# Three instructions reordered in the first dense block, six background VectorE jobs moved later

## The chip, the cores and the metric

The kernel runs on one core of one Trainium2 chip, as one program. Times are device microseconds (us) from the first to the last instruction of the run. The engines are TensorE (PE, with its weight loads as PEld), VectorE (DVE), ScalarE (ACT), GpSimd (POOL) and SyncE (SP, which only issues transfers here).

## The reference, cut to what matters

Three layers follow each other: an attention with two kinds of masks, a gated dense layer, and a layer that sends each token to one of eight experts.

```
scores = scale * np.matmul(q, k.transpose(0, 1, 3, 2))        # q, k, v: 4 x 8 x 576 x 64
scores = np.where(masks[None, :, :, :], scores, -1000000000.0)
attn = np.exp(scores - np.max(scores, axis=-1, keepdims=True))
attn = attn / (np.sum(attn, axis=-1, keepdims=True) + 1e-09)
x = np.matmul(attn, v)            # then laid out as 2304 tokens x 512
...
gate = 1.0 / (1.0 + np.exp(-(x @ w_gate)))                    # w_gate, w_val: 512 x 1536
val = x @ w_val
x = gate * val @ w_out                                        # w_out: 1536 x 512
...
h = np.maximum(xc[mask] @ w1[e], 0.0)                         # per expert e, tokens whose best gate is e
y[mask] = gate_w[mask, None] * (h @ w2[e])
out[do_compute] = xc + y
```

## The kernel before, in words

**Attention.** The work is cut into 32 parts (`NS` = 32, numbered t here): a pair of heads of one batch and half of its rows. A step t of the loop works on four parts at once. TensorE makes the scores of part t (`scores`) and turns the exponentials of part t-2 round (`flip`, L319), and applies v to part t-3 (`apply_v`, L335). VectorE takes the row maxima of part t (L291), adds up and inverts the row sums of part t-1 (L303, L304), copies one of the two turned tiles of part t-2 (`pT`, L321) and the result of part t-3 (L341 or L347). ScalarE makes the exponentials of part t-1 (L297) and copies the other turned tile (L323). GpSimd multiplies both tiles of part t-1 with the inverted sums (`norm`, L310, two instructions that follow each other), and then does one subtraction of two tiles of x (L413). In every second step one more pair of q and k is turned (`turn`, `turn_rest`).

The order in which a step issues its pieces is a string of letters, which is also the order on each engine. It is `eSfEmIFnaNDTMRpDAaL` for t < 32: e and E are the exponentials, S the scores, f and F the two flips with their copies, m and M the two maxima, I the sums and their inverse, n and N the two GpSimd multiplications, T and R the turns, A the application of v, L the loads. The letters D, a and p each take one job from the front of a background queue of VectorE, ScalarE and GpSimd. When the front job's inputs are not there yet, or the queue is empty, nothing is issued.

**Background jobs.** The dense layer multiplies float32 numbers as a high and a low part of each operand. `operand` queues, for each half of a tile of x, a ScalarE job (high part, L425) and a VectorE job that needs it (low part, `xl` = x - `xh`, L429, 128x384, both inputs in SBUF). In the last steps of the attention VectorE's queue holds only such low parts, for the first and second pair of token groups (p = 0 and 1).

**First dense block.** The dense layer runs over 12 blocks of columns (f) and 3 pairs of token groups (p). A block (`Block`) gathers seven products in four PSUM banks A, B, C and D, and each product (`mm`) is six matmuls (L558 to L560). `onto("C", "B")` copies bank B to bank C on ScalarE (L597), where the next product goes on adding; a fresh bank is written once by TensorE first (L564). `keep` copies B to SBUF (L590), `gate_of` takes a sigmoid (L601), `add_d` adds bank D (VectorE, L604). The first block (f = 0, p = 0, `first_period`) is spread over the last steps: each letter G issues one of its pieces. Those steps have strings of their own, for t = 32, 33 and 34 (`NS`, `NS + 1`, `NS + 2`). The rest follows as `period`, block by block, with no attention beside it.

Of the kernel before, what the change touches and what calls it, by code (L numbers as in the profile page):

```python
# [23 lines left out]
def kernel(  # L24
# [626 lines left out]
    def first_period(k):  # L651
        k.mm("A", "A11", "B11", True)
        yield
        k.onto("B", "A")
        k.mm("D", "S3", "T3", True)
        yield
        k.mm("B", "S2", "T2", False)
        k.keep("u2")
        yield
        k.mm("A", "A12", "B21", False)  # L660
        yield
        k.mm("B", "S1", "T1", False)
        k.gate_of("sA", "A")
        k.onto("C", "B")
        k.keep("u4")
        yield
        k.mm("C", "S4", "B22", False)
        k.add_d("u4")
        yield
        k.mm("D", "A22", "T4", False)  # L670
        k.gate_of("sC", "C")
        yield
        k.add_d("u2")
# [8 lines left out]
    NS = len(subs)  # L682
# [68 lines left out]
    def step_fill(t):  # L751
        if not first_block:
            blk0.append(Block(0, 0, lambda _: "X"))
            first_block.append(first_period(blk0[0]))
        next(first_block[0], 0)
# [53 lines left out]
        "D": lambda t: pop("D"), "a": lambda t: pop("A"), "p": lambda t: pop("P"),  # L809
    }  # L810
    ps_of = {}
    ORDERS = {NS: "LeAGEInNDfFapGDa", NS + 1: "LAGGfFGapDDaD", NS + 2: "LGAGGapDDa"}
    for t in range(NS + 3):
        for c in ORDERS.get(t, "eSfEmIFnaNDTMRpDAaL"):
            steps_of[c](t)
# [79 lines left out]
    for f, p in BL:  # L895
# [17 lines left out]
        k = Block(f, p)  # L913
# [22 lines left out]
    def slab(shape, dt, name):  # L936
        return late.tile(shape, dt, tag="slab", bufs=NSLAB, name=name)
# [273 lines left out]
    for i in range(8):  # L1211
        k = (NU - 3) * NC + 6 + 3 * i
# [199 lines left out]
    with tc.For_i(SLOTS, top, 128):  # L1412
# [32 lines left out]
        for e in range(NE):  # L1445
# [21 lines left out]
            for kk in range(KD):  # L1467
                t = slab([128, F], F32, f"ow1{e}{kk}")
# [3 lines left out]
            for i in range(NF // 2):  # L1472
                t = slab([128, 2, DM], F32, f"ow2{e}{i}")
# [47 lines left out]
```

## Time and profile before

| what | value |
|---|---|
| median of 3 runs | 765.17 us (763.15 to 766.51) |
| the profiled execution | 766.11 us, its span 763.9 us |
| TensorE busy | 735.4 us, 96% of the span |
| VectorE, ScalarE, GpSimd busy | 500.7, 417.9, 211.1 us |
| mean granted TensorE clock | 0.992 |

A span counts from the first to the last instruction of the profiled execution; some 2 us lie around it. The attention reaches to about 120 us, the first dense block from there to 134 us, the rest of the dense layer to about 398 us.

### The profile page before, as it was taken

Reading aid. Unit: us, or ns where it says so; the run is one execution under the profiler, and the core shown is the slowest. Engines: PE = TensorE matmul, PEld = TensorE weight load, DVE = VectorE, ACT = ScalarE, POOL = GpSimd, SP = SyncE. Lnnn points to the kernel's source line nnn. Section 1 sums busy time; section 2 is a strip of 40 time slices with the busy share of each in tenths; the row PEclk is TensorE's granted clock in tenths of the full one; section 3 lists DMA queues with packets and bytes.
Section 4 is the critical chain, followed back from the end, with each engine's and each line's share of the span. In section 5 each row is a group of like instructions: output and inputs, shape, how many; then the busy total and the mean of one; then the engine's idle time right before and its main releaser. Section 6 shows DMA issues by size and latency. Waiting matters only on the chain. (4 is left out here: it accounts for less than half of the span.)

```text
span 763.9 us, 13894 instructions
## 1 busy us (share of the span) xinstructions
PE 735.4 (96%) x4773; PEld 670.9 (88%) x4773; DVE 500.7 (66%) x1139; ACT 417.9 (55%) x1153; POOL 211.1 (28%) x233
## 2 busy tenths in 40 slices
PE   8999998999999999999999999999999899999993
PEld 5766666999999999999989999999988788888882
DVE  3799997978877777778656244345555766666540
ACT  5788886755555555555455233344445665566630
POOL 6677976000000000000010020210222755556510
PEclk9999999999999999999999999999999999999997
DMA  9999611243344443443456934626633667777600
GB/s 207 223 210 212 143 32 29 96 146 128 128 149 149 135 144 122 155 139 121 156 182 208 301 122 130 204 94 218 234 124 120 225 244 249 242 227 226 208 16 13
DMA packets 115795, 122.47 MB, mean 160 GB/s; under 512 B 58167, under 2 KB 90679, under 8 KB 115720
## 3 DMA queue, kind: packets, MB, share of 16 engines
q1 hardware_dynamic: 108952, 109.62, 47.2%
q0 software_dynamic: 4000, 8.51, 3.2%
q10 hardware_dynamic: 2768, 3.41, 1.3%
q8 instruction: 39, 0.64, 0.3%
q14 instruction: 36, 0.29, 0.1%
HBM read 90.78 MB, written 36.59 MB: 167 GB/s over the span
## 5 line engine op out<-in xcount | busy, mean ns | idle before, releaser
L558 PE MATMUL psX<-gt,wo 128*128 128x384 f32 x288 | 98.5, 342 | 1.2 <-DVE sl L1144 1.2
L559 PE MATMUL psX<-gt,wo 128*128 128x384 f32 x288 | 96.8, 336 | 0.3
L560 PE MATMUL psX<-gt,wo 128*128 128x384 f32 x288 | 96.4, 335 | 0.0
L609 POOL DMA_DIRECT2D gt<-sC x3 | 1.7, 568 | 256.4 <-DVE sC L607 256.4
L297 ACT ACTIVATE sm<-psX,mx 96x128 f32<-96x128 f32 (+2 forms) x176 | 61.8, 375 | 10.3 <-DVE mx L291 8.0
L310 POOL TENSOR_TENSOR sm<-sm,rs 96x384 f32<-96x384 f32 (+2 forms) x64 | 55.5, 887 | 32.3 <-DVE rs L304 20.3
L604 DVE TENSOR_TENSOR u<-psD,u 128x384 f32<-128x384 f32 x70 | 38.7, 553 | 36.1 <-PE psD L560 34.9
L558 PEld LDWEIGHTS psX<-gt,wo 128*128 128x128 f32 x288 | 54.2, 188 | 1.7 <-DVE sl L1144 1.5
L559 PEld LDWEIGHTS psX<-gt,wo 128*128 128x128 f32 x288 | 54.2, 188 | 1.2 <-DVE gt L874 1.2
L560 PEld LDWEIGHTS psX<-gt,wo 128*128 128x128 f32 x288 | 54.1, 188 | 0.0
L560 PE MATMUL psA<-xhB,wl 128*128 128x384 f32 x140 | 47.0, 336 | 0.7 <-DVE wl L531 0.7
L560 PE MATMUL psD<-xhT,wl 128*128 128x384 f32 x140 | 47.0, 336 | 0.2 <-DVE wl L531 0.2
L990 ACT COPY row<-psY 128x256 f32<-128x256 f32 x36 | 13.4, 373 | 61.5 <-PE psY L988 50.8
L558 PE MATMUL psD<-xhT,wh 128*128 128x384 f32 x140 | 46.9, 335 | 0.0
L559 PE MATMUL psA<-xlB,wh 128*128 128x384 f32 x140 | 46.8, 334 | 0.0
L559 PE MATMUL psD<-xlT,wh 128*128 128x384 f32 x140 | 46.8, 334 | 0.0
L558 PE MATMUL psA<-xhB,wh 128*128 128x384 f32 x140 | 46.8, 334 | 0.0
L560 PE MATMUL psB<-xhT,wl 128*128 128x384 f32 x140 | 46.8, 334 | 0.0
L558 PE MATMUL psB<-xhT,wh 128*128 128x384 f32 x140 | 46.8, 334 | 0.0
L559 PE MATMUL psB<-xlT,wh 128*128 128x384 f32 x140 | 46.8, 334 | 0.0
L991 DVE TENSOR_REDUCE lp<-psY 128x10 f32<-128x40 f32 x36 | 7.2, 199 | 56.4 <-ACT row L990 56.4
L871 ACT CAST gt<-gt 128x384 fp32r<-128x384 f32 x72 | 35.5, 514 | 12.3 <-DMA gt<-gt 10.0
(770 smaller groups left out, 2245.5 us busy)
## 6 DMA issues: line engine op xcount, KB each, us to landing
w1r<-in_moe_w_dram SPq DMA_DIRECT2D x32, 512.0 KB, 5.1
w2r<-in_moe_w_dram SPq DMA_DIRECT2D x32, 512.0 KB, 3.7
gt<-gt SPq DMA_DIRECT2D x72, 192.0 KB, 4.1
gt<-sC SPq DMA_DIRECT2D x33, 192.0 KB, 2.4
gt<-sA SPq DMA_DIRECT2D x33, 192.0 KB, 1.9
wg<-in_moe_w_gate_dram SPq DMA_DIRECT2D x12, 512.0 KB, 4.0
wv<-in_moe_w_val_dram SPq DMA_DIRECT2D x12, 512.0 KB, 3.6
wo<-in_moe_w_out_dram SPq DMA_DIRECT2D x12, 512.0 KB, 3.9
```

The source lines that it names most:

```text
L297: nc.scalar.activation(sm[:n, w, 0:c], src[:, w, :], AF.Exp, bias=mx[:n, w:w + 1], accum_out=sums[:n, h, w:w + 1])
L310: nc.gpsimd.tensor_tensor(x, x, rs[:n, h, 0:m].rearrange("p (w o) -> p w o", o=1).to_broadcast([n, m, c]), op=ALU.mult)
L558: nc.tensor.matmul(ps, lhsT=whi, rhs=xhi, start=start, stop=False, skip_group_check=skip)
L559: nc.tensor.matmul(ps, lhsT=whi, rhs=xlo, start=False, stop=False, skip_group_check=skip)
L560: nc.tensor.matmul(ps, lhsT=wlo, rhs=xhi, start=False, stop=stop, skip_group_check=skip)
L604: nc.vector.tensor_tensor(self.tm[nm], self.ps["D"], self.tm[nm], op=ALU.add)
L609: eng.dma_start(gts[self.f][2 * self.p + i], self.tm[nm])
L871: nc.scalar.copy(t[:, 0, :].bitcast(F32R), t[:, 1, :])
L990: nc.scalar.copy(row[m][:, 256 * a:256 * a + 256].rearrange("p (c n) -> p c n", c=2), pr[:, :, 0:128])
L991: nc.vector.tensor_reduce(lp[:, m, a, :], pr[:, :, 128:NR].rearrange("p c (t n) -> p n c t", t=2), axis=AX.XY, op=ALU.add)
```

## The change

In the first dense block the sigmoid of bank A is issued behind the copy from B to C and behind the copy of B to SBUF. In the steps t = 26 to 31 the letter D between N and T is left out, so that each takes one VectorE job instead of two. The three last strings have four letters D more: t = 32 two, t = 33 and t = 34 one each.

```diff
@@ first_period
         k.mm("B", "S1", "T1", False)
-        k.gate_of("sA", "A")
         k.onto("C", "B")
         k.keep("u4")
+        k.gate_of("sA", "A")
         yield
         k.mm("C", "S4", "B22", False)
         k.add_d("u4")
@@
-    ORDERS = {NS: "LeAGEInNDfFapGDa", NS + 1: "LAGGfFGapDDaD", NS + 2: "LGAGGapDDa"}
+    LATE = "eSfEmIFnaNTMRpDAaL"
+    ORDERS = {t: LATE for t in range(26, NS)}
+    ORDERS.update({NS: "LeAGEInNDDfFapGDDa", NS + 1: "LAGGfFGapDDDaD", NS + 2: "LGAGGapDDDa"})
     for t in range(NS + 3):
         for c in ORDERS.get(t, "eSfEmIFnaNDTMRpDAaL"):
             steps_of[c](t)
```

On ScalarE, at the end of the fifth piece of the first block (psX are its banks A, B and C; u_00 is `u4`, sA and sC are the two sigmoids), the rows with - are before and those with + are after:

```order
 L323 COPY pT<-psY 108x324
+L597 COPY psX<-psX 128x384
+L590 COPY u_00_2378<-psX 128x384
 L601 ACT_TABLE_LOAD
-L601 ACTIVATE sA_2379<-psX 128x384
-L597 COPY psX<-psX 128x384
-L590 COPY u_00_2384<-psX 128x384
-L601 ACTIVATE sC_2411<-psX 128x384
+L601 ACTIVATE sA_2380<-psX 128x384
+L601 ACTIVATE sC_2410<-psX 128x384
 L425 CAST xhT_2440<-xT_1915 128x768
```

The table load of the sigmoid moves with it: both stand behind the two copies now.

On VectorE, the step t = 27 before, from the sums to the copy of part 26's turned tile in the next step (xl are the low parts):

```order
L303 TENSOR_SCALAR sums<-sums 96x6
L304 RECIPROCAL rs<-sums 96x6
L429 TENSOR_TENSOR xlT_1627<-xT_1505,xhT_1626 128x384
L291 TENSOR_REDUCE mx<-psX 96x3
L429 TENSOR_TENSOR xlT_1758<-xT_1646,xhT_1757 128x384
L341 COPY x_1510<-psY 128x192
L341 COPY x_2049<-psY 128x96
L321 COPY pT<-psY 128x288
```

The same place after the change:

```order
L303 TENSOR_SCALAR sums<-sums 96x6
L304 RECIPROCAL rs<-sums 96x6
L291 TENSOR_REDUCE mx<-psX 96x3
L429 TENSOR_TENSOR xlT_1627<-xT_1505,xhT_1626 128x384
L341 COPY x_1510<-psY 128x192
L341 COPY x_2047<-psY 128x96
L321 COPY pT<-psY 128x288
```

The low part between the inverse and the maximum is gone, the one behind the maximum stays, and the jobs come one place later in each of the six steps.

On VectorE, the steps t = 32 and 33 before, from the inverse of the last part to the first addition of the first block:

```order
L304 RECIPROCAL rs<-sums 108x6
L429 TENSOR_TENSOR xlT_2157<-xT_2046,xhT_2156 128x384
L321 COPY pT<-psY 126x252
L429 TENSOR_TENSOR xlT_2271<-xT_2176,xhT_2270 128x384
L347 COPY x_1511<-psY 128x14x6
L347 COPY x_2050<-psY 128x14x12
L321 COPY pT<-psY 108x324
L429 TENSOR_TENSOR xlT_2271<-xT_2176,xhT_2270 128x384
L604 TENSOR_TENSOR u_00_2384<-psX,u_00_2384 128x384
```

The same place after the change:

```order
L304 RECIPROCAL rs<-sums 108x6
L429 TENSOR_TENSOR xlT_1896<-xT_1777,xhT_1895 128x384
L429 TENSOR_TENSOR xlB_1963<-x_969,xhB_1962 128x384
L321 COPY pT<-psY 126x252
L429 TENSOR_TENSOR xlB_1963<-x_969,xhB_1962 128x384
L429 TENSOR_TENSOR xlB_2026<-x_970,xhB_2025 128x384
L347 COPY x_1511<-psY 128x14x6
L347 COPY x_2048<-psY 128x14x12
L321 COPY pT<-psY 108x324
L429 TENSOR_TENSOR xlB_2026<-x_970,xhB_2025 128x384
L429 TENSOR_TENSOR xlT_2154<-xT_2044,xhT_2153 128x384 x2
L429 TENSOR_TENSOR xlT_2266<-xT_2172,xhT_2265 128x384
```

Three low parts have become eight in this place, before the row L604 (the last of nine stands behind the second addition). One of the added ones stands ahead of the copy pT of 126x252, which part 30 needs before v can be applied to it. TensorE's and GpSimd's instructions and all transfers keep their order.

## Rows read from the trace of the kernel before

**Rows 1.** Busy time by stretch: length, PE, PEld, DVE, ACT, POOL, clock, DMA share, GB/s

```profile
97.00:121.00 24.00, 21.75 (x229) 15.48 (x229) 23.01 (x60) 20.48 (x96) 18.16 (x20) 1.00 0.09 26
134.00:398.00 264.00, 262.22 (x1504) 259.97 (x1503) 200.74 (x355) 142.74 (x278) 4.20 (x11) 1.00 0.41 136
```

**Rows 2.** TensorE's waits, 97 to 142 us: waiting row, releaser: total, times, longest

```profile
PE psY L319 <- POOL sm L310: 2.2, 8, 0.3
PE psX L558 <- ACT psX L597: 1.5, 1, 1.5
PE psY L335 <- DVE pT L321: 0.4, 1, 0.4
```

**Rows 3.** ScalarE in order of time: start, duration, instruction, [idle time before, releaser]

```profile
127.60 0.43 ACT L323 COPY pT<-psY 108x324 f32<-108x324 f32 x1 [1.18 <-PE psY L319]
128.05 1.28 ACT L601 ACT_TABLE_LOAD   x1
129.34 0.49 ACT L601 ACTIVATE sA<-psX 128x384 f32<-128x384 f32 x1
129.73 0.49 ACT L597 COPY psX<-psX 128x384 f32<-128x384 f32 x1
130.13 0.48 ACT L590 COPY u<-psX 128x384 f32<-128x384 f32 x1
```

**Rows 4.** TensorE in order of time at the same place

```profile
128.41 0.34 PE L564 MATMUL psX<-xhB,wh 128*128 128x384 f32 x1
130.27 0.44 PE L558 MATMUL psX<-xhB,wh 128*128 128x384 f32 x1 [1.52 <-ACT psX L597]
```

**Rows 5.** VectorE in order of time, step t = 27

```profile
105.50 0.19 DVE L304 RECIPROCAL rs<-sums 96x6 f32<-96x6 f32 x1
105.61 0.51 DVE L429 TENSOR_TENSOR xlT<-xT,xhT 128x384 fp32r<-128x384 f32 x1
106.04 0.55 DVE L291 TENSOR_REDUCE mx<-psX 96x3 f32<-96x384 f32 x1
106.51 1.50 DVE L429 TENSOR_TENSOR xlT<-xT,xhT 128x384 fp32r<-128x384 f32 x1
107.93 0.51 DVE L341 COPY x<-psY 128x192 f32<-128x192 f32 x2
```

**Rows 6.** GpSimd in order of time, step t = 27

```profile
105.86 0.95 POOL L310 TENSOR_TENSOR sm<-sm,rs 96x384 f32<-96x384 f32 x1 [1.08 <-ACT kq L254]
106.77 0.82 POOL L310 TENSOR_TENSOR sm<-sm,rs 96x384 f32<-96x384 f32 x1
107.56 1.31 POOL L413 TENSOR_TENSOR xT<-x,x 128x384 f32<-128x384 f32 x1
```

**Rows 7.** VectorE and GpSimd in order of time, step t = 29

```profile
114.08 0.56 DVE L429 TENSOR_TENSOR xlB<-x,xhB 128x384 fp32r<-128x384 f32 x1
114.19 0.92 POOL L310 TENSOR_TENSOR sm<-sm,rs 126x252 f32<-126x252 f32 x1
114.56 0.51 DVE L341 COPY x<-psY 128x192 f32<-128x192 f32 x2
```

**Rows 8.** VectorE in order of time, the sums of step t = 30

```profile
115.99 0.17 DVE L303 TENSOR_SCALAR sums<-sums 108x6 f32<-108x6 f32 x1 [0.27 <-ACT sm L297]
```

**Rows 9.** VectorE in order of time, steps t = 32 to 34

```profile
122.36 0.54 DVE L303 TENSOR_SCALAR sums<-sums 108x6 f32<-108x6 f32 x1
123.01 0.19 DVE L304 RECIPROCAL rs<-sums 108x6 f32<-108x6 f32 x1
123.11 0.52 DVE L429 TENSOR_TENSOR xlT<-xT,xhT 128x384 fp32r<-128x384 f32 x1
123.55 0.41 DVE L321 COPY pT<-psY 126x252 f32<-126x252 f32 x1
123.88 1.44 DVE L429 TENSOR_TENSOR xlT<-xT,xhT 128x384 fp32r<-128x384 f32 x1
...
130.65 0.56 DVE L604 TENSOR_TENSOR u<-psX,u 128x384 f32<-128x384 f32 x1 [1.99 <-ACT u L590]
```

**Rows 10.** GpSimd in order of time, step t = 32

```profile
124.18 0.72 POOL L310 TENSOR_TENSOR sm<-sm,rs 108x324 f32<-108x324 f32 x1
124.87 1.32 POOL L413 TENSOR_TENSOR xT<-x,xT 128x384 f32<-128x384 f32 x1
```

**Rows 11.** TensorE in order of time, v applied to part 30

```profile
124.02 0.65 PE L335 MATMUL psY<-pT,v 126*64 126x126 f32 x8 [0.40 <-DVE pT L321]
```

## The prediction

> **What bounds the kernel now.** I looked first at the busy times by stretch. From 134 us on TensorE is busy 262.22 of 264 us in the dense layer [rows 1], and its order there is not touched. So the change is worth what it moves the start of that stretch, and no more. Ahead of it, in the last attention steps (97 to 121 us), VectorE is busy 23.01 of 24 us and TensorE 21.75 [rows 1]: VectorE, or what VectorE waits for, sets the pace. Then TensorE's own waits: between 97 and 142 us it loses 1.5 us once to a ScalarE copy (L597), 0.4 us once to the copy pT of VectorE (L321), and 2.2 us in eight small waits on GpSimd's multiplications [rows 2]. The first two lie on the path, since from 120 us on TensorE goes through the first block in order and each of its waits delays all that follows. The timelines of the three places give the terms.
>
> **First part: the copy ahead of the sigmoid.** ScalarE is free when the pT copy ends at 128.03 and loads the sigmoid's table (1.28 us), does the sigmoid and only then the copy from B to C, from 129.73 to 130.22 [rows 3]. TensorE has written the fresh bank C at 128.41 + 0.34 = 128.75 and starts the next product at 130.27, 0.05 us behind the copy [rows 4]. With the copy first it starts at about 128.79, ends 0.49 us later, and TensorE goes on at 129.33: 0.94 us earlier. What now comes later is the sigmoid of A: the copy to SBUF (0.40 us from start to start, as L597's), the table load and the sigmoid follow, so it ends near 131.4 instead of 129.8. It has cover: its product is needed only behind the second addition, and the second sigmoid waited for its own matmuls anyway. Without that cover it would cost 1.6 us; I put it at nothing. This term is -0.94 us.
>
> **Second part: six low parts fewer in the steps.** The job left out takes 0.43 us from its start to the next instruction's (105.61 to 106.04) [rows 5]. Six of them would be 2.58 us if VectorE were simply full. It is not. The other job of the same step starts at 106.51 and takes 1.42 us to the next start for the same work [rows 5]; it ends 0.37 us after GpSimd's second multiplication, at 107.56 [rows 6]. So it stands until GpSimd is through with both, and what it stands for is released by VectorE's own inverse (L304, 105.50): 0.36 us later GpSimd starts, 1.70 us later it has done both, 0.37 us later VectorE is free. The removed job lies inside that stretch. Without it the second one asks 0.43 us earlier and waits 0.43 us longer. What is left is that the removed job also held up GpSimd: the first multiplication takes 0.91 us to the second, the second 0.79 to the next, so 0.12 us per such step.
>
> The Trainium skill says as much ("SBUF — State Buffer", section "Who interferes with whom"): a VectorE instruction with two inputs in SBUF and a GpSimd instruction that reads SBUF exclude each other for a whole instruction, and the one that issues second is blocked. The 1.42 us against 0.43 agrees. But by that rule the waiting job would follow the first multiplication, at 106.77, and the step would be some 0.8 us shorter; the row shows that it waited for the second as well.
>
> The steps are not alike. In step 29 the job asks at 114.08, just 0.11 us before GpSimd's second multiplication, goes between the two (VectorE is on at 114.56, and the second multiplication takes 0.92 us) [rows 7]. Step 31 has the same form. Asked 0.43 us earlier it would no longer meet that gap: the second multiplication would start 0.12 us earlier, at 114.07, take some 0.6 us (an estimate: 0.92 less the 0.3 that the job held it up), and the job would end 0.37 us behind it, at about 115.05, 0.5 us later than now. In step 28, which has one more VectorE instruction in between, the earlier job would come into the gap instead and win up to 0.9 us (in step 27's numbers: 106.77 - 0.12 + 0.37 = 107.02 instead of 107.93); but two steps on ScalarE is the last, since the sums at 115.99 waited 0.27 us for its exponentials [rows 8], and it would keep most of that. I add: 0.12 us each in steps 26, 27 and 30, 0.2 from step 28, and 0.5 lost each in 29 and 31. The first loss falls into the wait for ScalarE; the second into the sums of step 32, which take 0.54 us instead of the 0.17 of step 30 [rows 8, 9], so there is 0.37 us of cover. That leaves 0.36 + 0.2 - 0.13, about 0.4, of which I take half, -0.2 us at the end of step 31, because the waits shift too. The bounds are +1.0 (both losses in full, nothing won) and -2.6 (six full jobs).
>
> **Third part: the jobs come back in the tail.** Most are free: VectorE is idle for 1.99 us ahead of the first addition [rows 9], and three or four jobs of 0.43 fit. But one of the two added in step 32 stands ahead of pT of part 30, and that copy is waited for: it starts at 123.55 [rows 9], and TensorE's product with v starts at 124.02 with 0.40 us of idle time [rows 11]. Cases for this job. It starts right behind the first one: +0.43 us, to which the product with v adds nothing else. Or GpSimd, which waits for the first job, gets in: then the second stands like the job at 123.88, which took until after GpSimd's second multiplication (1.36 us to the next start; that multiplication ends at 124.87 [rows 10]). Then pT starts at 124.87 + 0.37 = 125.24 instead of 123.55: +1.69. Or it gets between the two multiplications: 124.18 + 0.37 = 124.55, +1.00. No row shows two such VectorE jobs in a row with GpSimd waiting; GpSimd's two in a row did keep VectorE out [rows 5, 6], and if VectorE's two do the same it is the first case. I take +0.43 and keep +1.69 as the bound. TensorE has no wait between that product and the copy of the first part, so the two add up.
>
> **Sum.** -0.94 - 0.2 + 0.43 = -0.7 us on a profiled execution of 766.11 (span 763.9), that is 765.4. The median of the runs is 765.17, 0.94 us below that one, so I predict 764.5 us. Some 0.5% (3.8 us) is what a measurement of this kernel can tell from no change; this is a fifth of it.
>
> **Rivals.**
> - *GpSimd gets in during step 32*: -0.94 - 0.2 + 1.69 = +0.55, 765.7 us, a little slower than before. For it: L429 rows that came during a GpSimd multiplication were stopped for both. Against it: the job in question follows another of VectorE, not a wait. It decides from the point at which pT is more than 1.14 us late.
> - *It gets between the two multiplications*, as the job of step 29 does now [rows 7]: -0.94 - 0.2 + 1.00 = -0.14, 765.0 us. Against it: the job at 123.88 came 0.30 us before the second multiplication and did not get in [rows 9, 10].
> - *VectorE is simply full*: the six jobs' 2.58 us come off the steps in full, because the waiting jobs get in between the multiplications: -2.58 - 0.94 + 0.43 = -3.1, 762.1 us. For it: 23.01 of 24 us busy. Against it: the 1.42 us of waiting inside that number, and the exponentials that are late already in step 30. The rule of the Trainium skill named above ("SBUF — State Buffer", section "Who interferes with whom"), with the lock given up behind each instruction, leads to this case.
> - *Slower by more*: steps 29 and 31 lose their gap in full and GpSimd gets in during step 32: -0.94 + 1.0 + 1.69 = +1.75, 766.9 us. It decides from 0.94 us of lost gaps and late pT together.
> - *The copy is not freed*: if something else ends last at that place, the first term is nothing and the sum is +0.2 or more, 765.4 us. The rows show no other wait there.
>
> **How the numbers follow.** Chances: forecast 0.42, GpSimd in 0.25, between 0.12, VectorE full 0.12, slower by more 0.05, copy not freed 0.04. The cases lie between 762.1 and 766.9; the three runs before spread over 3.4 us, so a median adds about 1 us either way. The range 762.6 to 766.7 leaves out most of the full gain and the worst case, less than 2 in 10. No case reaches 761.3 or 769.0, the bounds of 0.5%, without the scatter of runs: faster 0.04, same 0.95, slower 0.01.
>
> **What would show it.** The wait of 1.5 us on L597 shrinks to about 0.6 and the copy starts within 0.1 us of the fresh bank's write. The L429 row behind the maximum stays at 1.4 to 1.9 us in steps 27 and 30, and GpSimd's first multiplication shrinks to the second's 0.82. In step 32 two L429 rows of 0.43 us stand ahead of pT, and TensorE's wait on pT grows from 0.40 to 0.6 or more. The first row of the dense layer's full stretch moves by less than 1 us. I am wrong if the L429 rows in the steps fall to 0.5 us (then the steps shorten and the gain is 2 to 3 us), or if a new wait appears on TensorE behind the late sigmoid, or in the blocks after 134 us.

## The result and the profile after

The changed kernel takes **767.72 us** (767.00 to 770.72, 9 runs), the kernel before 764.41 us on the same chip (763.15 to 766.66, 9 runs): a ratio of **1.0053, with a 95% interval of 1.0038 to 1.0067**. It is slower, by some 4 us. The forecast was 764.5 us with a range to 766.7, so the prediction was wrong in size and in sign. The profiled execution took 767.72 us, its span 765.6.

TensorE's waits between 97 and 142 us, as in [rows 2] (waiting row, releaser: total, times, longest):

```profile
PE psY L335 <- DVE pT L321: 4.0, 1, 4.0
PE psX L558 <- ACT psX L597: 0.6, 1, 0.6
```

The second wait fell from 1.5 to 0.6 us, as forecast. The first, for the copy pT of part 30, grew from 0.4 to 4.0 us. VectorE in order of time, steps 32 to 34, answers to [rows 9]:

```profile
122.03 0.19 DVE L304 RECIPROCAL rs<-sums 108x6 f32<-108x6 f32 x1
122.13 0.51 DVE L429 TENSOR_TENSOR xlT<-xT,xhT 128x384 fp32r<-128x384 f32 x1
122.57 3.67 DVE L429 TENSOR_TENSOR xlB<-x,xhB 128x384 fp32r<-128x384 f32 x1
126.16 0.41 DVE L321 COPY pT<-psY 126x252 f32<-126x252 f32 x1
...
134.86 0.56 DVE L604 TENSOR_TENSOR u<-psX,u 128x384 f32<-128x384 f32 x1
```

The added low part ahead of pT takes 3.67 us where a free one takes 0.5. pT starts 4.13 us behind the inverse (126.16 - 122.03), before it was 0.54 (123.55 - 123.01): 3.59 us later. What the low part stands for is in GpSimd's rows of the same time, which answer to [rows 10]:

```profile
122.39 0.85 POOL L310 TENSOR_TENSOR sm<-sm,rs 108x324 f32<-108x324 f32 x1 [0.49 <-ACT psX L597]
...
123.19 0.72 POOL L310 TENSOR_TENSOR sm<-sm,rs 108x324 f32<-108x324 f32 x1
...
123.88 0.99 POOL L413 TENSOR_TENSOR xT<-x,xT 128x384 f32<-128x384 f32 x1
...
124.83 0.99 POOL L413 TENSOR_TENSOR xT<-x,x 128x384 f32<-128x384 f32 x1
...
125.78 1.31 POOL L413 TENSOR_TENSOR xT<-x,x 128x384 f32<-128x384 f32 x1
```

Five instructions follow each other without a pause. The low part asked at 122.57, inside the first, and four went by. It ran in front of the fifth, whose row is 0.32 us longer than the two ahead of it. Before the change the first subtraction had the long row of 1.32 us [rows 10], so there VectorE came in ahead of the third instruction. That is a first reading; the runs below test it.

The busy times by stretch (columns as in [rows 1]) and three rows of TensorE show a second loss behind the first:

```profile
97.00:121.00 24.00, 21.86 (x225) 15.37 (x223) 22.70 (x55) 20.85 (x99) 18.95 (x21) 1.00 0.09 27
121.00:126.60 5.60, 1.64 (x9) 1.32 (x9) 5.47 (x6) 0.75 (x2) 5.11 (x6) 0.88 0.00 0
126.60:130.00 3.40, 3.38 (x15) 3.06 (x16) 1.89 (x4) 0.02 (x1) 0.49 (x1) 0.50 0.00 0
134.00:398.00 264.00, 261.93 (x1511) 260.10 (x1511) 201.82 (x358) 146.31 (x285) 3.23 (x6) 1.00 0.43 141
```

```profile
126.62 1.11 PE L335 MATMUL psY<-pT,v 126*64 126x126 f32 x8 [3.98 <-DVE pT L321]
...
128.15 0.52 PE L559 MATMUL psX<-xlT,wh 128*128 128x384 f32 x1
128.47 0.52 PE L560 MATMUL psX<-xhT,wl 128*128 128x384 f32 x1
```

While TensorE stood for 3.98 us the granted clock fell, and from 126.6 to 130.0 it was 0.50, that is 1.2 GHz. Matmuls of 384 columns that start 0.17 us apart at full clock are 0.32 us apart here. From the product with v to the write of the fresh bank C (L564) it took 6.91 us after (133.53 - 126.62), 4.39 before (128.41 - 124.02): 2.52 us more.

The copy from B to C, ScalarE and then TensorE in order of time, answers to [rows 3, 4]:

```profile
133.97 0.46 ACT L597 COPY psX<-psX 128x384 f32<-128x384 f32 x1 [0.83 <-PE psX L564]
134.34 0.49 ACT L590 COPY u<-psX 128x384 f32<-128x384 f32 x1
134.84 1.28 ACT L601 ACT_TABLE_LOAD   x1
136.14 0.49 ACT L601 ACTIVATE sA<-psX 128x384 f32<-128x384 f32 x1
```

```profile
133.53 0.34 PE L564 MATMUL psX<-xhB,wh 128*128 128x384 f32 x1
134.48 0.45 PE L558 MATMUL psX<-xhB,wh 128*128 128x384 f32 x1 [0.61 <-ACT psX L597]
```

The next product starts 0.95 us behind the fresh bank's write, against 1.86 before (130.27 - 128.41): 0.91 us won.

So the sum of the changed places is +3.59 + 2.52 - 0.91, and -0.27 from the steps (below): +4.93 us. On 764.41 us the interval of the ratio is +2.9 to +5.1 us, and the sum lies in it; the medians differ by 3.3 us. The two spans differ by 1.7 us only (765.6 - 763.9). The rest of the +4.93 went in places that the change does not touch: the execution after the change reached the inverse of step 25 earlier by 0.70 us (96.75 against 97.45), and from the dense layer's last matmul into bank D (391.51 before, 395.73 after) to the end it took 369.9 us against 372.4. Over all traces here that last stretch takes 367.7 (e7) to 374.0 us (e4), and its granted clock is not the same either: from 600 to 620 us it was 0.91 before and 1.00 after. No run ties this scatter to the change.

### The profile page after: what moved, and what is told of

Same layout as the page of the kernel before. It is cut to its first block, busy times and chain, and to the rows that moved or that the text cites. A ratio compares the mean times of both kernels' runs of the same rounds, so it can differ in the third digit from the quotient of the medians.

```text
span 765.6 us, 13899 instructions
## 1 busy us (share of the span) xinstructions
PE 734.9 (96%) x4771; PEld 671.4 (88%) x4773; DVE 499.4 (65%) x1139; ACT 417.0 (54%) x1153; POOL 210.9 (28%) x233
## 5 line engine op out<-in xcount | busy, mean ns | idle before, releaser
L604 DVE TENSOR_TENSOR u<-psD,u 128x384 f32<-128x384 f32 x70 | 38.8, 554 | 36.1 <-PE psD L560 34.8
```

Of the source, the lines that this page charges most:

```text
L604: nc.vector.tensor_tensor(self.tm[nm], self.ps["D"], self.tm[nm], op=ALU.add)
```

## The experiments

Start-up differs by up to 1.4 us from one execution to the next, and the last layer by more, so places are compared by distances inside one trace: from the inverse (L304) of step 25 to that of step 32 (the steps), and from there to the second addition (L604) of the first block (the tail). "Run" is how many GpSimd instructions follow each other without a pause in step 32. "Low part that waits" is the duration of the second low part of that step, "wait on pT" TensorE's wait for the copy. Columns three to six are in us.

| kernel | run | low part that waits | wait on pT | steps | tail | median, ratio to before (95%) |
|---|---|---|---|---|---|---|
| before | 3 | behind pT | 0.4 | 25.55 | 10.59 | |
| after | 5 | 3.67 | 4.0 | 25.28 | 15.79 | 767.72, 1.0053 (1.0038 to 1.0067) |
| e1 copies first | 3 | behind pT | 0.4 | 25.53 | 9.68 | 763.36, 1.0003 (0.9981 to 1.0025) |
| e2 orders only | 5 | 3.67 | 4.0 | 25.26 | 16.69 | 769.09, 1.0072 (1.0048 to 1.0095) |
| e3 job behind pT | 5 | behind pT | 0.4 | 25.28 | 10.57 | 761.92, 0.9977 (0.9958 to 0.9997) |
| e4 one ahead of pT | 3 | 1.77 | 2.1 | 25.54 | 13.82 | 768.42, 1.0041 (1.0020 to 1.0063) |
| e5 cut to three | 3 | 1.77 | 2.1 | 25.27 | 11.43 | 764.43, 1.0012 (0.9990 to 1.0033) |
| e6 cut to two | 2 | 1.08 | 1.4 | 25.28 | 10.69 | 763.48, 0.9991 (0.9972 to 1.0010) |
| e7 wait filled | 5 | 3.68 | 0.8 left | 25.27 | 13.29 | 766.58, 1.0024 (1.0001 to 1.0047) |
| e8 early job kept | 5 | behind pT | 0.4 | 24.06 | 10.59 | 761.42, 0.9962 (0.9944 to 0.9980) |
| e9 and the old tail | 5 | behind pT | 0.4 | 24.07 | 9.67 | 761.62, 0.9973 (0.9952 to 0.9995) |

**One part of the change at a time.** e1 is the kernel before with the sigmoid moved alone.

> Only the first part of the change: both copies ahead of the sigmoid, all orders of the steps as before. Theory (port): the loss comes from the second job ahead of pT alone, so this part gives its 0.9 us: TensorE's wait on L597 falls from 1.5 to about 0.6 us, no other wait grows, median about 763.5. Rival (late sigmoid): the sigmoid that comes later holds something up behind it, and the median is 764.4 or more with a new wait of TensorE after 130 us.

The tail is 0.91 us shorter and the wait on L597 0.6 us. The place is as forecast; 0.9 us is less than the median can tell. e2 is the changed kernel with the sigmoid back in its old place.

> Only the orders of the steps and of the tail as in the change, the sigmoid ahead of the copies as before. Theory (port): TensorE's wait of 4 us on pT and the low clock behind it stay, the wait on L597 is 1.5 us again, median about 768.6 (0.9 above the changed kernel). Rival (late sigmoid): the loss goes with the first part, and the median is that of the kernel before, about 764.

The wait of 4.0 us and the half clock are there without the moved sigmoid, and the tail is 0.90 us longer than after. So the loss belongs to the orders. e3 takes one letter out of its place:

```diff
-NS: "LeAGEInNDDfFapGDDa"
+NS: "LeAGEInNDfFapGDDDa"
```

> The changed kernel with one letter moved: in step 32 the second job stands behind the copy pT and the first-block piece instead of ahead of pT. Theory (port): TensorE's wait on pT falls from 4.0 us to 0.5 or less, the clock stays at 2.4 GHz, and what the steps (0.9 us) and the copy (0.9 us) win is left: dense layer 1.5 to 2 us earlier than before, median about 762.6. Rival (the jobs as such are too many for the tail): a wait of about the same size turns up at the next place where VectorE is waited for, median 767 or more.

One low part issued behind pT instead of ahead of it takes the whole loss away, and the interval of its ratio ends just below 1 (0.9997). The expectation of a dense layer 1.5 to 2 us earlier was a miss: the steps gave 0.27 us and not 0.9, and the tail is that of before (10.57 against 10.59), 0.29 us in all. What the median has beyond that stands in no place that was compared. VectorE's rows say why: the same low part still stands for GpSimd (3.38 us), but the copy that TensorE needs is no longer behind it. There is a new wait of TensorE, 0.8 us for the addition L604, which has four low parts ahead of it where there was one; it takes back what the earlier copy won:

```profile
129.57 1.48 DVE L429 TENSOR_TENSOR xlT<-xT,xhT 128x384 fp32r<-128x384 f32 x3
130.98 0.54 DVE L604 TENSOR_TENSOR u<-psX,u 128x384 f32<-128x384 f32 x1
```

e4 is the opposite: the kernel before, with one D more ahead of pT in step 32 (`"LeAGEInNDDfFapGa"`) and nothing else.

> The kernel before with one of its own jobs moved ahead of pT in step 32, nothing else changed, and no job added. Theory (port): that L429 stands for 3 us or more behind GpSimd's two multiplications and two subtractions, TensorE waits about 4 us on pT and runs at the low clock for some us, median about 768.5 (4 above before). Rival (the number of deferred jobs, or the inputs of just that job in the changed kernel): the job takes 0.4 to 1.7 us, TensorE waits at most 2 us, median 766 or less.

Slower, as expected, but by a different wait, the one that the rival named: the low part took 1.77 us and TensorE waited 2.1, not 4. GpSimd pauses ahead of its second subtraction in this program, as in the kernel before, where that one starts 0.08 us behind the end of the first (124.87 + 1.32 = 126.19 [rows 10]):

```profile
126.27 1.01 POOL L413 TENSOR_TENSOR xT<-x,x 128x384 f32<-128x384 f32 x1
```

In both traces it waits there for a result of the first subtraction. In the changed program the same subtraction waits for a result of VectorE that is long there, and starts at 124.83 without a pause. The five in a row are thus an effect of the change too, one that its diff does not show; that it comes of another buffer for this subtraction is likely and not shown.

**What the low part waits for.** The theory "string": it gets in ahead of the last of a run. e5 puts a small GpSimd copy that has to wait for ScalarE behind the first subtraction, e6 ahead of it.

```diff
+    held = small.tile([128, 1], F32, tag="held", bufs=1, name="held")
+    steps_of["h"] = lambda t: nc.gpsimd.tensor_copy(held, blk0[0].tm["u2"][:, 0:1])
-NS + 1: "LAGGfFGapDDDaD"
+NS + 1: "LAGGfFGahpDDDaD"
```

> The changed kernel with one small GpSimd copy (one column of a bank's SBUF copy that ScalarE writes, its result unused) behind the first of the three background subtractions. It has to wait for ScalarE there, so that in step 32 GpSimd has only two multiplications and one subtraction in one go instead of two and three. Theory 'string' (a VectorE low part that asks while GpSimd is in a run of instructions that follow each other without a pause gets in just ahead of the run's last one): the second low part of step 32 gets in ahead of the first subtraction, takes 1.7 to 1.8 us instead of 3.67, TensorE waits about 2.1 us on pT instead of 4.0, and the median falls by some 2 to 4 us against the changed kernel, to about 764 to 766 us. Rival 'fixed hold' (it waits some fixed stretch, or until all work that GpSimd has queued there is done): 3.6 us or more and a wait of 4.0 us again, 767.7 us.

> As the run before, but the small copy stands ahead of the first subtraction, so that GpSimd's run without a pause in step 32 is the two multiplications alone (the subtractions come behind the pause). Theory 'string': the second low part of step 32 gets in ahead of the second multiplication, takes about 1.0 us, and TensorE waits about 1.3 us on pT; the median is 1 us or so below the run with the string of three, 763 to 765 us. Rival 'fixed hold': 3.6 us and a wait of 4.0 us again. A second rival, that the low part waits for both multiplications because they are of one line: 1.7 us or more and a wait of 2 us, as with the string of three.

Both as "string" has it. Of e5, the low part and the subtraction in front of which it ran; of e6, the low part and the second multiplication:

```profile
122.93 1.77 DVE L429 TENSOR_TENSOR xlB<-x,xhB 128x384 fp32r<-128x384 f32 x1
...
124.25 1.31 POOL L413 TENSOR_TENSOR xT<-x,xT 128x384 f32<-128x384 f32 x1
```

```profile
123.67 1.08 DVE L429 TENSOR_TENSOR xlB<-x,xhB 128x384 fp32r<-128x384 f32 x1
...
124.30 1.04 POOL L310 TENSOR_TENSOR sm<-sm,rs 108x324 f32<-108x324 f32 x1
```

The ones that are 0.32 us longer are the third and the second of the run. With the wait the loss goes: the tail falls from 15.79 to 11.43 and 10.69 us, and both intervals take in 1.

**The clock's share.** e7 fills TensorE's wait with thirty matmuls (`busy(30, pv)` ahead of the product with v of part 30).

> The changed kernel with thirty additional matmuls of 252 columns (their result is overwritten) on TensorE right ahead of the application of v to part 30, where TensorE waits 4.0 us for pT. They fill most of that wait and change nothing else. Theory: part of the loss is the clock, which was granted at 0.50 from 126.6 to 130.0 us after TensorE had stood still. Then with the wait filled the clock stays at 1.00 there, the matmuls behind it are about 0.17 us apart instead of 0.32, pT comes no earlier, and some 2 us of the 4.2 come back: 765.5 us. Rival: the clock cost nothing, or something else (GpSimd, ScalarE) sets the pace behind the wait: 767.7 us as before.

Stretches of e7, the filled one and the one behind it:

```profile
123.42:127.57 4.15, 3.40 (x31) 2.85 (x30) 4.15 (x4) 0.00 (x0) 4.15 (x5) 1.00 0.00 0
127.57:132.00 4.43, 4.43 (x33) 4.21 (x33) 3.04 (x7) 0.91 (x2) 0.47 (x1) 1.00 0.01 4
```

pT is as late as before, the clock stays at 1.00, and from the product with v to the write of bank C it is 4.41 us again. The tail is 2.50 us shorter than after. The median came down by 1.1 us only (by the ratios 2.2), and the two intervals overlap; the 2.5 us rest on the trace.

**The other low part of the steps.** The change left out the low part between N and T. e8 is e3 with the other one left out (`LATE = "eSfEmIFnaNDTMRpAaL"`).

> The kernel that beat both (no second low part ahead of pT in step 32), with the other one of the two low parts left out of steps 26 to 31: the one between the two multiplications' letters stays, and the one behind the maximum goes. Theory: the low part that stands 1.4 to 2 us in steps 26, 27, 28 and 30 is the one that asks while GpSimd is in its multiplications; the one that stays asks ahead of them and takes 0.43 us. So VectorE's steps become shorter by up to 0.9 us each until ScalarE's exponentials or TensorE bind, and the median is 760 to 761 us against 761.9. Rival: the steps are bound by ScalarE or by GpSimd's multiplications after all, 762 us, no difference.

The steps fall to 24.06 us, 1.49 less than before and 1.22 less than with the change's choice. VectorE at the inverse of step 27 and on to the sums of step 28 in e8:

```profile
103.88 0.19 DVE L304 RECIPROCAL rs<-sums 96x6 f32<-96x6 f32 x1
103.98 0.51 DVE L429 TENSOR_TENSOR xlT<-xT,xhT 128x384 fp32r<-128x384 f32 x1
...
107.43 0.17 DVE L303 TENSOR_SCALAR sums<-sums 96x6 f32<-96x6 f32 x1 [0.40 <-ACT sm L297]
```

The low part right behind the inverse asks before GpSimd begins and takes 0.51 us. The sums now wait for ScalarE's exponentials, so ScalarE takes over part of the bound. The medians of e3 and e8 can't be told apart. e9 is e8 with the three last strings as before the change.

> The kernel of the run before last in this list that kept the early job of steps 26 to 31, with the three last strings as they were before the change (four letters D fewer; the jobs left over come behind the second addition of the first block) and with the copies ahead of the sigmoid. Theory: the distance from VectorE's inverse of step 25 to that of step 32 stays at 24.06 us (25.55 in the kernel before); from there to the second addition of the first block it falls from 10.59 to 9.68 us, as with the copies alone, because no low parts stand ahead of the first addition, and the wait of 0.8 us on L604 goes. Sum against before: -1.49 - 0.91 = -2.4 us; median 760.5 to 761.5 us and below the kernel that kept the early job (761.42). Rival: the low parts that come later now (six behind the second addition) hold up the two products of the gate behind them or the next block's additions, and the 0.9 us are lost again there: 761.4 us or more.

Steps and tail are as forecast (24.07 and 9.67), but the median is that of e8, as the rival said. The medians can't tell 0.9 us, and the traces say that the rival holds in part. TensorE's waits of e9 between 97 and 142 us have a new one, for low parts of the weights, which stand behind the low parts of x that came later (e8 waits 0.3 us for one there). From the first matmul behind the tail to the dense layer's last one into bank D e9 took 257.76 us and e8 257.38, so some 0.4 of the 0.9 us were lost again.

```profile
PE psA L560 <- DVE wl L531: 0.7, 1, 0.7
```

**How long a run can keep VectorE out.** In seven more runs the changed kernel has GpSimd instructions added in step 32 (results unused); e14 and e15 also have a copy that makes GpSimd pause behind them. e10 was to make the run six.

> The changed kernel with one more GpSimd subtraction (128x256, two inputs in SBUF, its result unused) right behind the third background subtraction, so that GpSimd's run in step 32 has six instructions without a pause instead of five. Theory 'string': the second low part of step 32 gets in ahead of the added subtraction and not ahead of the third background one, so it takes one subtraction more, 3.67 + 0.96 = about 4.6 us, and TensorE waits 4.9 to 5.0 us on pT instead of 4.0; the median rises by about 1 us against the changed kernel, to 768.5 to 769 us. Rival 'four and no more' (GpSimd lets VectorE in after its fourth instruction, whatever follows): 3.67 us and 4.0 us again, 767.7 us.

The median came out as expected, 768.62 us (1.0066, 1.0043 to 1.0088), and for another reason. The added instruction kept a buffer in use that the second subtraction needs, and GpSimd paused:

```profile
131.16 1.96 POOL L413 TENSOR_TENSOR xT<-x,x 128x384 f32<-128x384 f32 x2 [5.44 <-DVE xlB L429]
```

That was a run of three again, the low part took 1.65 us, TensorE waited 2.1 us and the clock fell; then three low parts stood 2.8 us for the added instruction ahead of the first addition, and TensorE waited 1.7 us for that one. e11 and e12 add without that side effect, one tiny subtraction and two of 128x128:

> What the run with the longer string was meant to be, without its side effect. There the added instruction read the first token group's x and so kept that buffer, which the second background subtraction needs; GpSimd paused ahead of it (5.44 us on a VectorE low part) and the run without a pause was one of three. Here the added subtraction reads the same x as the third one (one column of it, its result unused), and no wait is added. Theory 'string': the run has six instructions, the second low part of step 32 gets in ahead of the added one and behind the third background subtraction: 3.67 + 0.95 = about 4.6 us, TensorE waits 4.9 us on pT, the median is about 1 us above the changed kernel's ratio of 1.0053, near 1.0065. Rival 'four and no more': 3.67 us and 4.0 us again. Rival 'size': the added instruction is too short to matter, 3.67 us again.

> As the run before, with two added subtractions of 128x128 (results unused, different buffers), so that the run without a pause has seven instructions. Theory 'string': the low part gets in ahead of the last, behind the third background subtraction and the first added one. A 128x256 subtraction took 0.73 us and a 128x384 one 1.00, so one of 128x128 takes about 0.45 and the low part 3.67 + 0.95 + 0.4 = about 5.0 us; TensorE waits about 5.3 us on pT. Rival 'four and no more': 3.67 us and 4.0 us. Rival 'five and no more': 4.6 us and 4.9 us, as with six.

Both 3.67 us and 4.0 us (767.91 us, 1.0055, 1.0025 to 1.0084; 768.07 us, 1.0039, 1.0013 to 1.0064): "string" failed. In both, VectorE came in ahead of the third background subtraction with one or two instructions still behind it. e11's row of it:

```profile
126.60 1.30 POOL L413 TENSOR_TENSOR xT<-x,x 128x384 f32<-128x384 f32 x1
```

e13 to e15, one execution each, put short subtractions elsewhere:

> The changed kernel with two added GpSimd subtractions of 128x128 (constant inputs, results unused) between its two multiplications and its three background subtractions of step 32: a run of seven without a pause, norm, norm, short, short, sub, sub, sub. With runs of two, three and five the second low part got in ahead of the last; with six and seven it got in ahead of the fifth as well (3.67 us in all of them). Theory 'four': at most four GpSimd instructions pass while VectorE waits, counted from the one in which it asked. Then the low part gets in ahead of the first background subtraction and takes 0.66 + 0.69 + 2 x 0.4 + 0.5 = about 2.5 us, TensorE waits about 2.8. Theory 'time': it is let in at the first end of an instruction after about 2.3 to 2.9 us of waiting. Then it gets in behind the first background subtraction, about 3.5 us. Theory 'last of the run': ahead of the third background subtraction, 4.4 us or more.

> The changed kernel with one added subtraction of 128x128 (constant inputs, result unused) behind the first background subtraction, and a small copy that waits for ScalarE behind that: a run of four, norm, norm, sub, short, then a pause. Ahead of the last: the low part gets in ahead of the short one, 0.66 + 0.69 + 0.95 + 0.43 = about 2.7 us, TensorE waits about 3.0 us. By a count of four alone (with nothing on the last one) it would come behind the short one, 3.1 us or more.

> The changed kernel with six added subtractions of 128x8 (constant inputs, results unused) behind the two multiplications of step 32 and a small copy that waits for ScalarE behind them: a run of eight, of which the last six are tiny, about 0.15 us each. By 'four' the low part gets in ahead of the third tiny one, and that one is the one that GpSimd starts late or that takes longer. By 'time' (2.3 us or more) no limit is reached and the run's last instruction decides: it gets in ahead of the sixth tiny one, about 0.45 us later. By 'last of the run' the same. The low part takes 1.35 + 0.3 + 0.43 = about 2.1 us in the first case and 2.5 in the other.

None of the three theories. The low part took 1.13 us in e13, 1.77 in e14 and 1.08 in e15 (761.57, 763.87 and 763.48 us, one run each; the one run of the kernel before beside them took 768.55, so these times alone tell little). GpSimd in e13, the second multiplication and the first short one:

```profile
123.09 1.08 POOL L310 TENSOR_TENSOR sm<-sm,rs 108x324 f32<-108x324 f32 x1
...
124.14 0.39 POOL L815 TENSOR_TENSOR held<-ident 128x128 f32<-128x128 f32 x1
```

VectorE came in ahead of the second multiplication although five instructions followed it without a pause. In all five runs with added short subtractions that did not pause (e11 to e15) the low part got in ahead of the instruction in front of the first added one, as if that one were a pause. e16 and e17 ask whether it is their being added or their size: one added subtraction of 128x384, behind the three or ahead of them.

> The changed kernel with one added GpSimd subtraction of full size (128x384, the same inputs as the third background one, its result into a tile that nothing reads any more) behind the third background subtraction: a run of six. In the run of six with a tiny added instruction the low part got in ahead of the third background subtraction (3.67 us). Theory 'four': again there, 3.67 us, a wait of 4.0 us. Theory 'only a short instruction ends the run early' (small added ones acted like a pause): the low part gets in ahead of the added one, about 4.6 us, and TensorE waits about 4.9 us.

> As the run before, with the added full-size subtraction between the two multiplications and the three background subtractions: norm, norm, added, sub, sub, sub. Theory 'four': the low part gets in ahead of the second background subtraction, 0.66 + 0.69 + 0.95 + 0.95 + 0.42 = 3.67 us. Theory 'an added instruction ends the run' (as with the two short ones, where it got in ahead of the second multiplication): 1.1 us, a wait of 1.4 us. Theory 'ahead of the last, if none is short': 4.6 us, a wait of 4.9 us.

Both took 4.62 us and TensorE waited 4.9 us (769.17 and 768.09 us, one run each). e16, the low part and the added sixth instruction; then e17's last subtraction:

```profile
123.43 4.62 DVE L429 TENSOR_TENSOR xlB<-x,xhB 128x384 fp32r<-128x384 f32 x1
...
127.59 1.31 POOL L814 TENSOR_TENSOR busy_in<-x,x 128x384 bf16<-128x384 f32 x1
```

```profile
126.75 1.31 POOL L413 TENSOR_TENSOR xT<-x,x 128x384 f32<-128x384 f32 x1
```

Five full-size instructions went by in each. There is no limit of four, and none of 3 us. In step 32 "ahead of the last of the run" holds wherever nothing short was added, in runs of two, three, five and six. It is no rule for all instructions of the kernel's own sizes. In steps 29 and 31 of the kernel before, with multiplications of 126x252, the low part got in ahead of the second of three: in step 29 that second one ends at 114.19 + 0.92 = 115.11 [rows 7], and the third follows without a pause:

```profile
115.07 0.99 POOL L413 TENSOR_TENSOR xT<-x,xT 128x384 f32<-128x384 f32 x1
```

With nothing in between that multiplication takes 0.60 us, less than those of step 32 (0.72). Why a short instruction ends the wait as a pause does stays open.

## Why the prediction was wrong

**First part, the copy: right.** -0.94 us forecast, -0.91 measured in after and in e1; the wait is 0.6 us, as said, and the late sigmoid delayed nothing.

**Second part, the steps: right in size, in part by luck.** -0.2 us forecast, -0.27 measured. From inverse to inverse the steps 26, 28 and 30 are 0.14, 0.13 and 0.12 us shorter, the 0.12 us of the prediction or near it; step 27 won nothing (its first multiplication still takes 0.95 us), and step 31 lost 0.08 (the sums behind it, at 121.02, took 0.90 us where they took 0.54). The remaining low part of step 27 took 1.97 us at 105.20, longer than the 1.50 of [rows 5], as said. The losses counted for steps 29 and 31 did not come in the way that was foreseen: there the low part, asked earlier, ran ahead of the first multiplication (0.55 us at 112.65 and at 119.34) and made that one 0.4 us longer (1.14 against 0.74). That the sum was halved "because the waits shift" was a guess. What the prediction did not see is that the low part to leave out is the one behind the maximum: e8 won 1.49 us with as many jobs.

**Third part, the step that failed: the second job ahead of pT.** The prediction chose "It starts right behind the first one: +0.43 us" and kept "+1.69 as the bound". It measured +3.59. The choice was wrong, and the bound as well. It took as the worst case a wait until the end of GpSimd's second multiplication, because in [rows 5, 6] the waiting low part went ahead of the third instruction. But in that step the third instruction was the last of a run, and nothing in those rows tells "two multiplications" from "all but the last"; the one row with another outcome, in step 29 [rows 7], has shorter multiplications. In step 32 three background subtractions stand behind the multiplications, and the changed program took away the pause that parted them. e4, with that pause left, measured 1.69 us (pT 2.23 us behind the inverse instead of 0.54), the bound as stated. So the rival "GpSimd gets in" had the mechanism, and its price was that of the unchanged program's run of three. The price of the rival "between the two multiplications", +1.00, is what e6 measured for its run of two (pT 1.55 us behind the inverse, +1.01).

The rule named in the prediction (the Trainium skill, "SBUF — State Buffer", "Who interferes with whom") has the second one blocked while the other holds the shared ports for a whole instruction. The traces agree that the two exclude each other, and not that the lock is free again behind each instruction: four went by in after, five in e16. Only where the short ones of steps 29 and 31 before and of e11 to e15 stood did VectorE get in earlier than ahead of the last.

The prediction asked whether two VectorE jobs in a row keep GpSimd out. In step 32 they did not: GpSimd asked during the first low part and got in ahead of the second. But VectorE's run can do it. In e5 a subtraction that takes 1.0 us when free asked at 128.66, four low parts went by (128.74 to 130.70), and it was over at 131.57:

```profile
128.66 2.91 POOL L413 TENSOR_TENSOR xT<-x,x 128x384 f32<-128x384 f32 x1
128.74 0.55 DVE L429 TENSOR_TENSOR xlB<-x,xhB 128x384 fp32r<-128x384 f32 x1
129.21 1.49 DVE L429 TENSOR_TENSOR xlT<-xT,xhT 128x384 fp32r<-128x384 f32 x3
```

**What had no term at all: the clock.** A longer wait was priced at its own length. The wait of 4.0 us cost 2.52 us more in matmuls at 1.2 GHz (e7 gave 2.50 back). That is half of the +4.93. The price is not fixed: behind the same wait e11 took 1.43 us more (5.82 against 4.39).

The chance of 0.01 for slower by over 0.5% came from cases that all ended below 767 us; the bound of the third part carried that error.

## What to carry to other kernels

Price a VectorE instruction with two SBUF inputs, issued beside GpSimd work that reads SBUF, at up to the whole run of GpSimd instructions that follow without a pause, all but the last (less where short ones stand in it), and look in the changed program, not in the old one, for where that run ends. Put it behind what others wait for, or ahead of GpSimd's start: moving one low part by one place was worth 5.2 us in the tail, and choosing which of two to drop 1.2 us in the steps. A wait that makes TensorE stand for microseconds is to be priced with matmuls at half clock behind it: here 1.4 to 2.6 us behind 4.0 to 4.9 us, and 0 or 1.6 us behind 2.1.

## What the runs showed of the hardware

The clock did not answer to the wait's length alone. With waits of 4.0 and 4.9 us on pT it fell to 0.50 in all traces here (after, e2, e11, e12, e16, e17); with 1.4 us or less it stayed at 1.00 (before, e1, e6, e13, e15), and so it did behind the 1.5 us on L597 before. How long it stayed low differed: to the write of bank C it took 6.9 to 7.0 us in after, e2, e12 and e16, 6.31 in e17 and 5.82 in e11. With 2.1 us it fell in e4, e10 and e14, which took some 1.6 us more to the write of bank C (5.94 to 5.98 us against 4.39), and stayed in e5. The stretch of the same kind in e4 and e5:

```profile
125.80:128.80 3.00, 3.00 (x12) 2.70 (x9) 0.61 (x2) 0.37 (x1) 1.96 (x2) 0.50 0.16 55
```

```profile
126.00:130.00 4.00, 3.81 (x25) 3.45 (x23) 2.63 (x7) 1.01 (x3) 2.44 (x3) 1.00 0.00 0
```

Both had waited 2.1 us. What else decides is not known.
